# Attention with a gated FFN on one core: part of the third unit's row maxima by rectified differences on ScalarE, the last unit in halves, and another order table

## The chip, the cores and the metric

The kernel runs on one core of a Trainium2 chip. The metric is the device time of one execution in microseconds. Engines are named as in the profile: PE (TensorE), ACT (ScalarE), DVE (VectorE), POOL (GpSimd), SP (SyncE, which only issues DMAs here).

## The reference

A layer norm without weights, attention of 32 heads of 16 columns over 2048 rows, and a gated FFN on the raw input, summed with the input. `B_x` is not used.

```python
x = A_x                                   # [1, 2048, 512] bf16
xn = _layernorm(x, axis=-1)
# _A_ref: qkv = xn @ wqkv, 32 heads of 16
scores = jnp.einsum("bhqd,bhkd->bhqk", q, k) * (Dh ** -0.5)
p = _softmax(scores, axis=-1)
o = jnp.einsum("bhqk,bhkd->bhqd", p, v)   # then @ wo
# _B_ref: (silu(x @ w1) * (x @ w3)) @ w2, 1792 columns in between
return x + _A_ref(xn, A_wqkv, A_wo) + _B_ref(xn, B_w1, B_w3, B_w2)
```

## The kernel before, in words

**Units.** The 2048 rows of queries are four chunks of 512, the 32 heads eight groups of four. For each chunk and group the rows are cut into units: 128, 128 and 256 rows in the first, 128 four times in the last four groups, 256 twice elsewhere (`UNIT_HEAD`, `UNIT_TAIL`). There are 73 units, numbered from 0. "The third unit" is unit 2 (256 rows, head group 0, chunk 0), the last is unit 72 (128 rows).

**First pass, the row maxima.** For every 128 rows and head (a row block) PE makes scores against 2048 keys as four tiles of 128 by 512, one PSUM bank each (L1476, four heads side by side in the row groups of the array). DVE reduces two banks at a time to two maxima (`tensor_reduce`, L1529) and puts them in `part`, an SBUF tensor with one set of columns for even units and one for odd units. When a unit's maxima are all there, `final_max` takes the greatest over the four key chunks, on DVE for the first two and the last units (L1688) and on POOL otherwise (six short steps from L1658 on), and writes its negative, split in two bf16 numbers, into `Z`. From there it becomes two more rows of the transposed queries `QT`: through PE and one copy by ACT or DVE (`tile_QT2`, L1135 and L1131, the units in `FAST_AUG`), or through a transposing DMA and two more DMAs. So the second pass subtracts the maximum inside the matmul.

**Twelve row blocks go another way** (`SPLITS`, kind "S" in the list `p1`). With a and b the scores of two key chunks, max(a, b) = b + relu(a - b). POOL writes the negated queries `QN` (L1552), PE adds a and -b up in one bank (`d_cand`, L1588, twice, for chunks 0 and 1 and for 2 and 3), ACT writes the Relu of each bank into the buffer `RB` (L1597; two at once in `exp_pair`), PE makes b alone for chunks 1 and 3, and one DVE instruction adds `RB` and takes the maximum of all 1024 columns (L1522). That is one DVE instruction of two banks for a row block where the plain way takes two. A split counts as 2 in the progress count `p1_n`, like the four plain tiles that it stands for (0.5 each).

**Second pass.** PE makes the transposed scores against the augmented queries (L1796, or as full-width products with the block-diagonal `BD`, L835), ACT takes the exponential out of one bank (L1821) or of two neighbouring banks at once (L1852, "a pair") into slots of `PT`, PE multiplies with the values and a column of ones (`tile_PV`, L839), ACT copies the result out (L1919), POOL and some DMAs divide by the sum; for the last four units DVE does that (L1901 to L1905).

**Around it.** At the head the input is normalised (statistics on DVE and ACT by `STATS`, the scaling on DVE at L902 or on POOL at L912 by `NORM`, for eight groups of 128 rows times two), transposed on PE, copied out by ACT (L944), and multiplied for keys, queries and values. The keys of head group 0 come as four chunks KT0_0 to KT0_3 (`tile_KT`, evacuated by ACT at L968). The other groups' keys go through DRAM in pairs of groups (`tile_heads`: kq L1023, spill L994, fetch L1011), each with a point of `p1_n` by which it is needed (`HEAD_K`, `LEAD_K`). The FFN's tiles, the output products and the stores fill in between.

**The order** of all instructions is worked out while the program is built: `_Prog` keeps a model of each engine's time, and a loop at the end of `_build` takes, of the best candidates of the five engines, the one that the model starts first. Which candidate is best hangs on some forty numbers in `RULES` (K). The count of work done is cut into stretches of 12 (`SEG`); `TUNE` names for each stretch an entry of `SETS`, whose numbers replace the defaults there. In the first pass `p1_cand` takes the blocks of units 0 to 2 in any order as their keys arrive (`N_HEAD`), and the rest in the order of the list. A DVE or ACT instruction waits for what it reads and writes through semaphores; each engine runs its own list in order.

**The tail.** The last unit's 16 tiles of exponentials wait for its maxima; its output rows then need PV (L839), the division on DVE, the last output products (L835) and a store (L1250). `HALVES` (by `NHALF`, 0 before) names units whose heads 2 and 3 have their maxima, their augmented queries and their exponentials ahead of those of heads 0 and 1 (`half_max`, `qt_half`).

Of the kernel before, what the change touches and what calls it, by code (L numbers as in the profile page):

```python
# [268 lines left out]
def _build(nc, A_x, A_wqkv, A_wo, B_w1, B_w3, B_w2, out):  # L269
# [29 lines left out]
    NHALF = 0  # L299
# [11 lines left out]
    FFN_HI = 880  # L311
# [3 lines left out]
    HEAD_K = 14  # L315
# [8 lines left out]
    NORM = "dddppppp"  # L324
    STATS = "daddddaa"
    W2_AT = 8
    R_STAT = 2
    R_SEC = 1
    SPLITS = ((20, 44, 2), (58, 58, 2))
# [3 lines left out]
        dict(),  # L333
        dict(P2_FRAG=0.0, URG_WAIT=0.05, A_LEAD=0.82, PAIR_WAIT=0.15),
        dict(PAIR_WAIT=0.15, RELAX=0.05),
        dict(ROW_LEAD=0.4, P2_NEAR=0.2),
        dict(A_LEAD=0.69, P1_EARLY=0.15, COUPLE=0.25),
        dict(TOL=0.1),
        dict(TOL=0.15, TEN_MID=2),
        dict(TOL=0.0, PV_LEFT=2, A_LEAD=0.55, AGAIN=3),  # L340
        dict(A_LEAD=0.88, HEAT_WIDE=0.34, URG_WAIT=0.05),
        dict(TOL=0.15, BD_NEAR=0.8),
        dict(BD_NEAR=0.5, HEAT_P1=0.35, P1_SLIP=0.3, LAZY_MAX=6.0),
        dict(PV_LEFT=2, BD_NEAR=0.1),
# [10 lines left out]
        dict(P1_SLIP=0.15, BD_NEAR=0.5, RELAX=0.05, HEAT_TILE=0.5),
        dict(PAIR_TEN=2, ROW_LEAD=0.5),
        dict(P1_SLIP=0.3),
        dict(BD_NEAR=0.2, OUT_GATE=20, TOL=0.1),
        dict(PV_LEFT=2, TOL=0.1, LAZY_MAX=6.0, W_WAIT=0.1),
        dict(PAIR_DEPTH=5, P1_SLIP=0.15, COUPLE=0.25),  # L360
        dict(P1_SLIP=-0.15, WIDE_LEAD=1.0),
        dict(HEAT_FILL=0.6, P1_SLIP=-0.15),
        dict(HEAT_FILL=0.82, W_WAIT=0.2, SP_RANK=1),
        dict(BD_NEAR=0.1, OUT_GATE=20, P1_SLIP=0.15, P2_MID=5),
        dict(RELAX=0.1, HEAT_TILE=0.7, P1_SAME=-0.1),
        dict(HEAT_FILL=0.42, MIN_PIECE=2, W_WAIT=0.2, P2_MID=5),
        dict(PAIR_WAIT=0.1, BD_NEAR=0.5),
        dict(MIN_PIECE=3, PAIR_DEPTH=2, P1_TRI=1, PAIR_TEN=2),
        dict(OUT_GATE=14, TOL=0.1),
        dict(MIN_PIECE=3, P1_TRI=1, PACE=3000),  # L370
        dict(PAIR_WAIT=0.05, HEAT_FORCE=0.34, ROW_LEAD=0.5),
        dict(A_LEAD=0.88, P2_FRAG=0.2, P2_NEAR=0.1, HEAT_FORCE=0.0),
        dict(TOL=0.0, URG_WAIT=0.05, RELAX=0.05, AGAIN=1),
        dict(A_LEAD=0.69, WIDE_LEAD=1.0),
        dict(PAIR_DEPTH=5, HEAT_TILE=0.5, PAIR_WAIT=0.15),
        dict(COUPLE=0.04, P2_MID=2),
        dict(TOL=0.05),
        dict(BD_NEAR=0.5, WIDE_LEAD=0.7),
        dict(A_LEAD=0.69, HEAT_P1=0.35, HEAT_WIDE=0.0, WIDE_LEAD=1.0),
        dict(LAZY_MAX=6.0, BD_NEAR=0.1),  # L380
        dict(MIN_PIECE=2),
        dict(A_LEAD=0.55, PV_LEFT=3, FILL_SLIP=0.1, TOL=0.03),
        dict(A_LEAD=0.69, HEAT_FILL=0.82, URG_WAIT=0.15),
        dict(HEAT_WIDE=0.3, PAIR_WAIT=0.1, LAZY_MAX=1.0, P1_SLIP=0.15),
        dict(BD_NEAR=0.8),
        dict(PAIR_WAIT=0.0, A_LEAD=0.6, LAZY_GAP=0.3, P1_SAME=0.05),
        dict(A_LEAD=0.55, P1_TRI=1),
        dict(W_WAIT=0.2, COUPLE=0.08, HEAT_WIDE=0.57),
        dict(HEAT_P1=0.35, AGAIN=4, FILL_SLIP=0.2),
        dict(ROW_LEAD=0.4, TOL=0.15),  # L390
        dict(HEAT_FORCE=0.46, TRI_WAIT=0.3),
        dict(COUPLE=0.25, P1_SAME=0.1, ROW_LEAD=0.5),
        dict(TOL=0.1, SP_RANK=1, P1_TRI=1, COUPLE=0.25),
        dict(RELAX=0.2, P1_SLIP=-0.15),
        dict(A_LEAD=0.55, URG_WAIT=0.15),
        dict(PAIR_WAIT=0.1, HEAT_P1=0.35, URG_WAIT=0.15, SP_RANK=1),
        dict(P1_SLIP=0.3, SP_RANK=1, ROW_LEAD=0.55, P2_MID=2),
        dict(TOL=0.03, WIDE_LEAD=0.7, P2_NEAR=0.4),
        dict(ROW_LEAD=0.43, WIDE_LEAD=0.7),
        dict(FILL_SLIP=0.2, W_WAIT=0.2),  # L400
        dict(HEAT_P1=0.0, HEAT_FILL=0.82),
        dict(MIN_PIECE=2, TOL=0.05, WIDE_LEAD=0.7, W_WAIT=0.1),
        dict(FILL_SLIP=0.1, W_WAIT=0.1, P2_NEAR=0.02, WIDE_LEAD=1.0),
        dict(ROW_LEAD=0.55, PV_LEFT=2, HEAT_FILL=0.7, PAIR_WAIT=0.0),
        dict(TOL=0.03, P2_NEAR=0.0),
        dict(WIDE_LEAD=0.7, SP_RANK=1),
        dict(A_LEAD=0.69, SP_RANK=1, RELAX=0.1),
        dict(HEAT_FILL=0.75, ROW_LEAD=0.55, COUPLE=0.08),
        dict(P1_TRI=1, A_LEAD=0.82, P1_EARLY=0.3, WIDE_LEAD=1.0),
        dict(BD_NEAR=0.2, HEAT_TILE=0.5, URG_WAIT=0.05),  # L410
        dict(URG_WAIT=0.15, P1_SLIP=-0.15),
        dict(HEAT_FORCE=0.5, P2_NEAR=0.02),
# [198 lines left out]
    with ctx:  # L611
# [1881 lines left out]
```

## Time and profile before

| what | value |
|---|---|
| time, median of 3 runs | 1180.53 us (1180.08 to 1181.3) |
| span of the profiled execution | 1178.6 us |
| mean granted TensorE clock | 0.998 |
| first reduction of maxima begins, last begins | 13.79 us, 1160.97 us |
| first exponential begins, last ends | 36.62 us, 1173.3 us |
| busy DVE, ACT, PE, POOL | 1165.0, 1158.5, 1111.9, 449.4 us |

How to read the profile: a line of the page or of a view has the kernel's line (L1529), the engine, the operation, output and input tensors, shapes, the count, then the busy time and the mean length of one in ns, then the idle time of that engine just before and what ended it. A timeline has start and length in us; where several instructions are merged ("x17") the length runs from the first start to the last end. Instructions of one engine overlap a little, so the spacing of starts is less than the length of one; the chain of waits has lengths by spacing. In the row of digits each is the busy share of a fortieth of the span, in tenths.

### The profile page before, as it was taken

To read this page: it belongs to the slowest core of one execution; us is meant where nothing else is said; L and a number is where in the kernel's file an instruction comes from. 1 tells how busy PE (TensorE), PEld (TensorE's weight loads), DVE (VectorE), ACT (ScalarE), POOL (GpSimd) and SP (SyncE) were. 2 spreads that over 40 slices of the span, in tenths; PEclk is the share of its full clock that TensorE was granted. 3 is DMA by queue.
4 is the path that set the end of the run, shared out by engine and by line. 5 is a ranking of instruction groups with operands and counts; after the bars stand their busy time and mean duration, and the time that the engine had idled before them with its cause. 6 is when DMAs were issued, how large, how long until landed. Compare 5 with 4: busy or idle time off the path is not lost.

```text
span 1178.6 us, 35702 instructions
## 1 busy us (share of the span) xinstructions
PE 1111.9 (94%) x14770; PEld 512.0 (43%) x14922; DVE 1165.0 (99%) x1089; ACT 1158.5 (98%) x2130; POOL 449.4 (38%) x886
## 2 busy tenths in 40 slices
PE   8999999999999999999989999999999999899988
PEld 4444334434344433334434444434444443356654
DVE  8999999999999999999999999999999999999996
ACT  8899999999999999999999999999999999999998
POOL 7245534244424246244432222455632126432211
PEclk9999999999999999999999999999999999999999
DMA  8323232111121121111110111221210121001001
GB/s 250 82 70 80 61 91 58 48 29 40 31 49 32 31 67 35 46 39 30 45 27 24 30 43 28 60 52 44 54 30 22 43 57 36 25 22 29 11 11 28
DMA packets 140966, 55.79 MB, mean 47 GB/s; under 512 B 103296, under 2 KB 140804, under 8 KB 140804
## 3 DMA queue, kind: packets, MB, share of 16 engines
q1 hardware_dynamic: 140804, 53.50, 17.7%
q8 instruction: 118, 1.93, 0.7%
q14 instruction: 44, 0.36, 0.1%
HBM read 38.93 MB, written 6.74 MB: 39 GB/s over the span
## 4 chain that ended last, share of the span: by engine, by line
ACT 55%; DVE 31%; PE 11%; issue 1%; DMA 0%; POOL 0%; ACTq 0%; SPq 0%
ACT PT L1821 35%; DVE part L1529 31%; ACT PT L1852 13%; PE ps L835 4%; PE ps L839 3%; PE ps L1796 3%; PE ps L1476 2%; ACT zg L1191 1%; ACT ub L1195 1%; ACT th L1185 1%; ACT RB L1597 1%; ACT U L1919 1%; ACT kq L1023 0%; DMA PT<-in_A_x_dram 0%; ACT osb L1264 0%
## 5 line engine op out<-in xcount | busy, mean ns | idle before, releaser
L1529 DVE TENSOR_REDUCE part<-ps 128x2 f32<-128x1024 f32 x1000 | 1133.9, 1207 | 0.4 <-PE ps L1796 0.2
L1821 ACT ACTIVATE PT<-ps 128x512 bf16<-128x512 f32 x1498 | 799.6, 660 | 2.6 <-PE ps L1796 2.0
L1796 PE MATMUL ps<-QT,KT 32*128 32x256 bf16 (+1 forms) x3768 | 455.1, 258 | 9.0 <-ACT PT L1852 2.8
L1476 PE MATMUL ps<-KT,QT 32*128 32x512 bf16 x2048 | 417.1, 383 | 5.6 <-DVE part L1529 2.1
L1852 ACT ACTIVATE PT<-ps 128x1024 bf16<-128x1024 f32 x275 | 292.2, 1097 | 0.2
L1796 PEld LDWEIGHTS ps<-QT,KT 32*128 32x128 bf16 x3768 | 167.2, 92 | 164.0 <-issue 71.5
L839 PE MATMUL ps<-PT,Vaug 128*17 128x256 bf16 (+1 forms) x4672 | 185.5, 261 | 5.0 <-ACT PT L1852 2.7
L835 PE MATMUL ps<-xnT,ident 128*128 128x512 bf16 (+3 forms) x569 | 151.9, 324 | 24.5 <-ACT PT L1852 7.3
L1476 PEld LDWEIGHTS ps<-KT,QT 32*128 32x128 bf16 x2048 | 104.4, 91 | 141.8 <-issue 59.4
L835 PE MATMUL ps<-xnT,w 128*128 128x512 bf16 (+3 forms) x542 | 141.5, 330 | 8.3 <-ACT U L1919 2.3
L1944 POOL TENSOR_TENSOR Rc<-Lc,mone 128x8 f32<-128x8 f32 (+1 forms) x69 | 104.8, 1519 | 91.6 <-DMA Lc<-U 91.6
L839 PEld LDWEIGHTS ps<-PT,Vaug 128*17 128x17 bf16 x4672 | 88.0, 89 | 75.6 <-issue 51.1
L835 PE MATMUL ps<-BD,KT 128*128 128x256 bf16 (+1 forms) x604 | 103.6, 262 | 0.9 <-ACT PT L1852 0.3
L1658 POOL TENSOR_TENSOR mx<-part 128x16 f32<-128x16 f32 (+1 forms) x60 | 14.2, 236 | 233.9 <-DVE part L1529 233.7
L835 PEld LDWEIGHTS ps<-xnT,ident 128*128 128x128 bf16 x626 | 49.2, 97 | 105.2 <-ACT PT L1821 37.6
L835 PE MATMUL ps<-w,hT 128*128 128x128 bf16 (+3 forms) x326 | 77.9, 304 | 2.3 <-issue 1.0
L1162 POOL TENSOR_SCALAR t<-th 128x512 f32<-128x512 bf16 x56 | 34.7, 620 | 100.8 <-ACT th L1185 99.2
L835 PEld LDWEIGHTS ps<-xnT,w 128*128 128x128 bf16 x584 | 43.1, 97 | 67.4 <-issue 33.3
L1166 POOL TENSOR_TENSOR hT<-a,t 128x512 bf16<-128x512 f32 x56 | 71.0, 1268 | 2.5
L1164 POOL TENSOR_TENSOR a<-zg,ub 128x512 f32<-128x512 bf16 x56 | 64.5, 1153 | 7.5 <-ACT ub L1195 7.5
L835 PEld LDWEIGHTS ps<-BD,KT 128*128 128x128 bf16 x604 | 50.6, 98 | 22.5 <-ACT PT L1852 2.2
L1980 POOL TENSOR_TENSOR on_b<-U,R 128x256 bf16<-128x256 f32 (+1 forms) x33 | 23.4, 710 | 93.6 <-DMA R<-rd 93.5
(114 smaller groups left out, 722.8 us busy)
## 6 DMA issues: line engine op xcount, KB each, us to landing
w<-in_B_w_dram SPq DMA_DIRECT2D x112, 128.0 KB
R<-rd SPq DMA_DIRECT2D x55, 128.0 KB
QT<-qd SPq DMA_DIRECT2D x31, 128.0 KB
KT<-kd SPq DMA_DIRECT2D x28, 128.0 KB
BD<-QT SPq DMA_DIRECT2D x220, 10.5 KB
xr<-in_A_x_dram SPq DMA_DIRECT2D x16, 128.0 KB
out_dram<-osb SPq DMA_DIRECT2D x16, 128.0 KB
qd<-kq SPq DMA_DIRECT2D x15, 128.0 KB
```

Of the source, the lines that this page charges most:

```text
L835: return e.matmul(bank(bk)[:, c0 + a:c0 + b], make_lhsT(0, 128), rhs_ap(0)[:, a:b], start=start, stop=stop, **kw)
L839: ins = e.matmul(bank(bk)[32 * i:32 * i + m, c0 + a:c0 + b], make_lhsT(i), rhs if (a, b) == (0, ncols) else rhs[:, a:b], start=start, stop ...
L1162: q.append(_Item(lambda e: e.tensor_scalar(t1[:, :], th[:, ss, :], 1.0, 1.0, ALU.mult, ALU.add), [("th", ss)], [("t1",)], 0.62, 0.72))
L1164: q.append(_Item(lambda e: e.tensor_tensor(a32[:, :], zg[:, ss, :], ub[:, ss, :], ALU.mult), [("zg", ss), ("ub", ss)], [("a32",)], 1.1, 1.25))
L1166: q.append(_Item(lambda e: e.tensor_tensor(hT[:, hslot(idx), :], a32[:, :], t1[:, :], ALU.mult), [("a32",), ("t1",)], [("hT", hslot(idx))] ...
L1476: ins = e.matmul(bank(held[i]), QT[32 * j:32 * j + 32, qs, q * 128:(q + 1) * 128], KT[32 * j:32 * j + 32, g, c_ * 512:(c_ + 1) * 512], sta ...
L1529: redq.append(_Item(lambda e: e.tensor_reduce(dst, banks, AX.X, ALU.max), writes, [("part", par, i_) for i_ in ix[:m]], _c_dve(512 * m), c ...
L1796: ins = e.matmul(bank(b)[:, i * nq:(i + 1) * nq], KT[32 * j:32 * j + 32, g, (k0 + i) * 128:(k0 + i + 1) * 128], QT[32 * j:32 * j + 32, qs, ...
L1821: expq.append(_Item(lambda e: e.activation(PT[:, sl, :], bank(b), ACTF.Exp, scale=SCALE), [("ps", b)], [("PT", sl)], _c_act(512), cb=cb, e ...
L1852: return _Item(lambda e: e.activation(PT[:, s0:s1 + 1:s1 - s0, :], two_banks(b0, b1), ACTF.Exp, scale=SCALE), [("ps", b0), ("ps", b1)], [( ...
L1944: poolq["nrm"].append(_Item(lambda e: e.tensor_tensor(Rc[:, pp, 0:nl], Lc[:, pp, 0:nl], mone[:, 0:nl], ALU.pow), [("Lc", pp), ("mone",)], ...
L1980: poolq["nrm"].append(_Item(lambda e: e.tensor_tensor(onorm[ob][:, oslot(ob, g), q0:q0 + nq], U[:, us, 0:nq], R[:, pp, 0:nq], ALU.mult), [ ...
```

## The change

- `SPLITS`: the twelve steady row blocks by differences are in units 14 to 47, every third, where they were in units 20 to 42, every second.
- `HEAD_SPLITS`: five of the eight row blocks of unit 2 go by differences too. They come last in that unit's list; the other three stay plain and in the head's free order. There are three more buffers beside `RB`, in slots of `hT` that the FFN fills later; `HEAD_LOOK` and `split_prep` let their differences start up to 24 and their negation up to 40 counts ahead. One negation serves all blocks of the same 128 rows.
- Unit 2's maxima have columns of their own in `part` (`side`).
- `NHALF` = 1: the last unit in halves.
- The fourth of eight normalisation groups is scaled on DVE, not POOL; `HEAD_K` 14 to 8; transposes and the first group's keys get the rank of the augmented queries on PE (`FIRST`). `KT_PARTS` only makes a number out of what was fixed before.
- A second tile may be open for PV when slots of `PT` run out (`PV_TEN`, 0 by default). `OUT_GATE` 14 to 10, `FFN_HI` 880 to 900.
- The model's length of a split's DVE instruction grows by 0.028 us.
- New `SETS` and `TUNE`.

```diff
-    NHALF = 0
+    NHALF = 1
...
-    FFN_HI = 880
+    FFN_HI = 900
...
-    HEAD_K = 14
+    HEAD_K = 8
...
-    NORM = "dddppppp"
+    NORM = "ddddpppp"
...
+    KT_PARTS = (0,)
+    FIRST = ("AQ", "tr", "KT0")
...
-    SPLITS = ((20, 44, 2), (58, 58, 2))
+    SPLITS = ((14, 50, 3),)
+    SPLIT_ROWS = 1
+    HEAD_SPLITS = {2: ((0, 0), (0, 1), (0, 2), (0, 3), (1, 0))}
+    HEAD_BUFS = (10, 14, 18)
+    HEAD_LOOK = 24
...
+        PV_TEN=0,
...
-        OUT_GATE=14,
+        OUT_GATE=10,
...
+    SPLIT.update(HEAD_SPLITS)
...
-        part = sb("part", [128, 2, 8 * NQC], FP32)
+        part = sb("part", [128, 3, 8 * NQC], FP32)
...
+            rbufs = [(RB[:, :, :], [("RB", 0), ("RB", 1)], [[("RB", 0)], [("RB", 1)]])]
+            for s_ in HEAD_BUFS:
+                rbufs.append((hT[:, s_:s_ + 4, :].rearrange("p a b -> p (a b)").bitcast(FP32)
+                              .rearrange("p (h n) -> p h n", n=512), [("hT", s_ + i) for i in range(4)],
+                              [[("hT", s_), ("hT", s_ + 1)], [("hT", s_ + 2), ("hT", s_ + 3)]]))
...
+        def side(u):
+            return 2 if u == 2 else u % 2
...
             for k, (qt, j) in enumerate(split):
+                if u in HEAD_SPLITS:
+                    ops.append(("S", u, qt, 0, j))
+                    continue
...
-        N_HEAD = sum(1 for b_ in p1 if b_[1] < 3)
+        N_HEAD = sum(1 for b_ in p1 if b_[1] < 3 and b_[0] == "R")
...
+        split_buf = [k % len(rbufs) if p1[n][1] in HEAD_SPLITS else 0 for k, n in enumerate(splits)]
...
-                par = u % 2
+                par = side(u)
...
+                    rb, rk, _ = rbufs[split_buf[splits.index(n)]]
                     redq.append(_Item(lambda e: e.tensor_tensor_reduce(
-                        out=RB[:, :, :], in0=banks, in1=RB[:, :, :], scale=1.0, scalar=-BIG,
+                        out=rb, in0=banks, in1=rb, scale=1.0, scalar=-BIG,
...
-                        _c_dve(1024) + 0.06, cb=fired, pred=lambda: split_done[n][0] == 2))
+                        writes + rk, rk + [("part", par, ix[0])],
+                        _c_dve(1024) + 0.088, cb=fired, pred=lambda: split_done[n][0] == 2))
...
+            ahead = 40 if u in HEAD_SPLITS else 16
...
-            if p1_at[n] - p1_n[0] > K.SPLIT_LOOK or (k and not split_done[splits[k - 1]][2]):
+            bf, kn = split_buf[k], split_of[k] % 2
+            if (p1_at[n] - p1_n[0] > (HEAD_LOOK if p1[n][1] in HEAD_SPLITS else K.SPLIT_LOOK)
+                    or any(split_buf[k_] == bf and not split_done[splits[k_]][2] for k_ in range(k))):
...
+            tenants = sum(b in bank_tenant for b in pool_banks())
+            if (p2_n[0] and red_n[0] < NP1 and tenants == K.TEN_MID and len(pt_free) <= K.PV_TEN and pv_ready()
+                    and not any(t.name.startswith("PV") for t in bank_tenant.values())):
+                bk = free_bank()[0]
...
-            return 0 if t.name.startswith("AQ") else 1.5 if t.name.startswith("V") else 2 if t.name.startswith("OUTB") else 1
+            return 0 if t.name.startswith(FIRST) else 1.5 if t.name.startswith("V") else 2 if t.name.startswith("OUTB") else 1
```

More of the change, by code (lines that the diff above doesn't have):

```diff
@@ L355, in _build @@
[L355 to L364, printed above, removed]
@@ L513, in _build @@
[L513 to L521 removed]
+        dict(COUPLE=0.18, HEAT_FILL=0.5),
@@ L599, in _build @@
     NU = len(units)
-    SPLIT = {u: ((units[u][3] // 128 - 1, 3),) for lo, hi, st in SPLITS for u in range(lo, hi, st)}
+    SPLIT = {u: tuple((units[u][3] // 128 - 1, 3 - r) for r in range(SPLIT_ROWS)) for lo, hi, st in SPLITS for u in range(lo, hi, st)}
+    SPLIT.update(HEAD_SPLITS)
     FAST_AUG = {0, 1} | set(range(NU - NFAST, NU))
@@ L952, in tile_KT @@
             groups = []
-            if sc == 0:
-                for t in range(XG):
+            if sc in KT_PARTS:
+                for t in range(4 * sc, 4 * sc + 4):
                     for c in range(DC):
@@ L971, in evac @@
                               cb=lambda op: done.add(("KT", 0, sc)), name="first")]
-            return _Tile("KT0_%d" % sc, groups, evac, cols=2048 if sc else 512,
+            return _Tile("KT0_%d" % sc, groups, evac, cols=512 if sc in KT_PARTS else 2048,
                          pred=lambda: "wk0" in done
-                         and all(("xnT", t) in done for t in range(sc * 4, sc * 4 + (4 if sc else 1))))
+                         and all(("xnT", t) in done for t in range(sc * 4, sc * 4 + (1 if sc in KT_PARTS else 4))))
         kq_free = list(range(NKQ))
@@ L1331, in _build @@
         NP1 = p1_at[-1]
-        N_HEAD = sum(1 for b_ in p1 if b_[1] < 3)
+        N_HEAD = sum(1 for b_ in p1 if b_[1] < 3 and b_[0] == "R")
+        assert all(b_[0] == "R" for b_ in p1[:N_HEAD])
         ug_n = {}
@@ L1544, in split_prep @@
             ug = qc * NG + g
-            if p1_at[n] - p1_n[0] > 16 or ("QT", ug) not in done or (i >= 2 and split_done[splits[i - 2]][1] < 2):
+            ahead = 40 if u in HEAD_SPLITS else 16
+            if (p1_at[n] - p1_n[0] > ahead or ("QT", ug) not in done or (u in HEAD_SPLITS and "QTb" not in done)
+                    or (i >= 2 and any(split_done[m_][1] < 2 for k_, m_ in enumerate(splits) if split_of[k_] == i - 2))):
                 return
@@ L1624, in final_max @@
             na = 4 * nqt
-            keys = [("part", par, i_) for i_ in range(NQC * na)]
-            p4 = part[:, par, 0:NQC * na].rearrange("p (k a) -> p a k", a=na)
+            keys = [("part", side(u), i_) for i_ in range(NQC * na)]
+            p4 = part[:, side(u), 0:NQC * na].rearrange("p (k a) -> p a k", a=na)
             ng = negm[:, par, 0:4 * nqt]
@@ L1653, in pool_max @@
                             1.0, 0.0, ALU.mult, ALU.add),
-                        [("part", par, i0)], [("part", par, i0 + na * c_) for c_ in range(1, 4)], 0.22))
+                        [("part", side(u), i0)], [("part", side(u), i0 + na * c_) for c_ in range(1, 4)], 0.22))
                 d2, m2 = mx[:, 0, 0:4 * nqt, :], mx[:, 1, 0:4 * nqt, :]
@@ L1695, in half_max @@
             par = u % 2
-            keys = [("part", par, 4 * c_ + j) for c_ in range(NQC) for j in js]
+            keys = [("part", side(u), 4 * c_ + j) for c_ in range(NQC) for j in js]
             h = slice(js[0], js[-1] + 1)
-            p4 = part[:, par, 0:4 * NQC].rearrange("p (k a) -> p a k", a=4)[:, h, :]
+            p4 = part[:, side(u), 0:4 * NQC].rearrange("p (k a) -> p a k", a=4)[:, h, :]
             ng = negm[:, par, h]
```

388 lines of the change are left out of this document (197 added, 191 removed), and 24 rows, old and new, of the table TUNE.

## The prediction

> **What bounds the kernel now.** I read the page first, then the busy time by stretch, the groups by shape, the two ends of the span as timelines, and the chain of waits.
>
> ```profile
> PE 1111.9 (94%) x14770; PEld 512.0 (43%) x14922; DVE 1165.0 (99%) x1089; ACT 1158.5 (98%) x2130; POOL 449.4 (38%) x886
> DVE  8999999999999999999999999999999999999996
> ACT  8899999999999999999999999999999999999998
> L1529 DVE TENSOR_REDUCE part<-ps 128x2 f32<-128x1024 f32 x1000 | 1133.9, 1207 | 0.4 <-PE ps L1796 0.2
> L1821 ACT ACTIVATE PT<-ps 128x512 bf16<-128x512 f32 x1498 | 799.6, 660 | 2.6 <-PE ps L1796 2.0
> L1852 ACT ACTIVATE PT<-ps 128x1024 bf16<-128x1024 f32 x275 | 292.2, 1097 | 0.2
> ```
>
> Two engines are full. DVE spends nearly all of it on one thing, the row maxima: 1000 reductions of two banks each, with 0.4 us of idle time ahead of all of them. ACT spends it on exponentials, 1498 of one bank and 275 of two. So the question is which of the two ends later once work is moved between them, and where each has holes.
>
> ```profile
> 25.00:35.00 10.00, 9.95 (x63) 3.82 (x62) 9.96 (x11) 5.94 (x10) 8.08 (x9) 1.00 0.59 187
> 35.00:60.00 25.00, 24.20 (x257) 11.66 (x264) 24.97 (x24) 22.96 (x45) 2.27 (x11) 1.00 0.30 77
> 60.00:100.00 40.00, 39.00 (x528) 17.95 (x529) 40.00 (x36) 39.19 (x72) 19.79 (x33) 1.00 0.28 68
> 100.00:500.00 400.00, 379.88 (x4609) 161.47 (x4649) 400.00 (x359) 398.48 (x714) 162.94 (x305) 1.00 0.20 50
> 500.00:1100.00 600.00, 568.50 (x7501) 262.02 (x7575) 599.76 (x542) 598.14 (x1108) 226.30 (x457) 1.00 0.15 37
> 1100.00:1173.30 73.30, 66.43 (x1655) 41.82 (x1665) 66.91 (x79) 73.00 (x137) 13.62 (x28) 1.00 0.08 17
> 1173.30:1178.60 5.30, 2.07 (x19) 0.59 (x20) 1.79 (x5) 0.00 (x0) 0.00 (x0) 0.55 0.07 25
> ```
>
> The columns after the stretch are its length and the busy time of PE, PE's weight loads, DVE, ACT and POOL, then the granted clock. ACT's holes are length minus busy: 4.06 us in 25 to 35, then 2.04, 0.81, 1.52, 1.86 and 0.30, 10.59 us in all until its last exponential at 1173.3. DVE has 0.31 us from 25 to 1100. The final 5.3 us hold only the last unit's products, its division and the store; nothing in the change touches them.
>
> ```profile
> 1160.97 1.21 DVE L1529 TENSOR_REDUCE part<-ps 128x2 f32<-128x1024 f32 x1
> 1164.11 0.28 DVE L1131 TENSOR_SCALAR QT<-ps 128x128 bf16<-128x128 f32 x1
> 1164.30 2.00 ACT L1852 ACTIVATE PT<-ps 128x1024 bf16<-128x1024 f32 x2
> 1169.35 3.92 ACT L1852 ACTIVATE PT<-ps 128x1024 bf16<-128x1024 f32 x4
> ```
>
> The last maximum ends at 1162.2, its result stands in QT at 1164.4, and the ACT timeline from 1164.30 on has eight pairs and three singles, 19 tiles, the last unit's 16 and three left over. ACT had about one microsecond of backlog when DVE delivered, so the two limits now coincide: **DVE sets the pace, and ACT is only about 1 us from setting it itself.** A change has to move both.
>
> **The change, part by part.** *Five row blocks of the third unit by rectified differences.* A row block is four maxima over 512 columns, two of L1529's reductions. The other way, in use on twelve blocks now, takes two one-bank Relus on ACT and one two-bank sum with maximum on DVE.
>
> ```profile
> 15.11 19.22 DVE part L1529 x17
> 676.90 10.78 ACT PT L1821 x22
> 222.73 3.67 ACT PT L1852 x4
> ```
> ```profile
> 366.10 1.21 DVE L1522 CUSTOM_DVE_ANT_0 RB<-ps,RB 128x1024 f32<-128x1024 f32 x1
> 367.24 0.08 DVE L1522 DVE_READ_ACCUMULATOR2_ANT part<- 128x1 f32 x1
> 367.24 2.35 DVE L1529 TENSOR_REDUCE part<-ps 128x2 f32<-128x1024 f32 x2
> L1597 ACT ACTIVATE RB<-ps 128x512 f32<-128x512 f32 x24 | 15.3, 646 | 0.1
> ```
>
> Instructions overlap, so I use spacings, not durations. A reduction takes 19.22/17 = 1.131 us of DVE; the split's one takes 367.24 - 366.10 = 1.14, and the next reduction starts while its accumulator is read. Per block DVE saves 2 x 1.131 - 1.14 = 1.12 us, for five 5.6. A one-bank ACT operation takes 10.78/22 = 0.49 us, a pair 3.67/4 = 0.917; the Relus have the shape of the exponentials, so ten cost 4.9 us (4.6 if all pair up).
>
> [...]
>
> Where do they lie? At the head, where ACT has its largest hole.
>
> ```profile
> 18.76 0.69 ACT L968 ACTIVATE KT<-ps,kbias 128x512 bf16<-128x512 f32 x1
> ...
> 30.08 0.69 ACT L968 ACTIVATE KT<-ps,kbias 128x512 bf16<-128x512 f32 x1 [0.69 <-PE ps L835]
> ...
> 36.62 1.02 ACT L1852 ACTIVATE PT<-ps 128x1024 bf16<-128x1024 f32 x1
> ```
> ```profile
> 50.65 0.24 POOL L1658 TENSOR_TENSOR mx<-part 128x16 f32<-128x16 f32 x1 [13.05 <-DVE part L1529]
> 50.98 0.20 POOL L1659 TENSOR_SCALAR mx<-mx 128x16 f32<-128x16 f32 x1
> ```
> ```profile
> 54.96 0.65 SPq L994 DMA_DIRECT2D kd<-kq  x1
> ...
> 58.01 1.44 SPq L1011 DMA_DIRECT2D KT<-kd  x2
> ```
>
> The second of the four key chunks is there at 19.5, so five first halves (2.5 us) can go into the hole of 25 to 35; the second halves need the fourth chunk. It comes at 30.8 and the first exponential at 36.6, so they go between. I take the hole as wholly filled: 4.06 of the 4.9 us are covered and 0.84 us are added to ACT. Without that cover all 4.9 would be added.
>
> The new wait: a split's sum needs both Relus, and DVE runs in order, so every later maximum queues behind it, and with it the banks those maxima hold on PE. The blocks come last in the unit and four buffers allow four at work, so I cost it at nothing, with at most one Relu spacing (0.49 us) for each of the last two as upper bound. PE gets six 512-column products per block where it had four: ten more at 0.37 us (below), side by side in row groups, against 0.8 us of PE idle in 35 to 60; they displace filling. POOL gets one more negation and five small copies ahead of the third unit's maxima, 0.33 us each by the spacing of the two steps above; it sat idle 13.05 us before that point.
>
> *Own columns for the third unit* remove no wait that the rows show (0.4 us before 1000 reductions), so zero; both ends of the bound are within that 0.4.
>
> *Fourth normalisation group on DVE, not POOL, and the head's ranks and key needs.*
>
> ```profile
> L902 DVE TENSOR_SCALAR osb<-PT,U 128x512 bf16<-128x512 bf16 x6 | 2.2, 407 | 0.0
> 25.38 1.52 POOL L912 TENSOR_SCALAR osb<-PT,U 128x512 bf16<-128x512 bf16 x2
> L1476 PE MATMUL ps<-KT,QT 32*128 32x512 bf16 x2048 | 417.1, 383 | 5.6 <-DVE part L1529 2.1
> ```
>
> DVE gets two of these, 2 x 2.2/6 = 0.7 us. POOL, which normalises until 26.9, is relieved of two (1.5 us) and two coefficient steps, so the fourth key chunk and the first exponential can come up to 1.5 us earlier, or not at all if ACT's other work holds them. I take no gain: an earlier start only shortens the hole that the Relus fill.
>
> The third unit's maxima end 5.6 - 0.7 = 4.9 us earlier, at about 45.7, and its exponentials can begin as much earlier, while ACT still has the 32 tiles of the first two units; that covers most of ACT's 2.85 us of holes in 35 to 100. What is late next is the second group's last key chunk: the fourth unit needs it 12 reductions (13.6 us) after its start, at 64.2 now and at 59.3 afterwards. Its load is issued at 58.01 and, going by the 3.05 us from its spill's issue (54.96) to its own, lands by 61.1. Left there, DVE would lose up to 1.8 us, of the gain and not beyond it; with HEAD_K at 8 these loads are due six steps (6.8 us) sooner, so I take zero.
>
> *Last unit in halves.* Only eight tiles wait for the last maximum, not sixteen: four pairs, 4 x 0.917 = 3.7 us off DVE's limit. It adds one small reduction (0.18 us, below) and one more copy like that of 1164.11 (0.28), on ACT or DVE. ACT's own limit does not move by it.
>
> ```profile
> 34.34 0.18 DVE L1688 TENSOR_REDUCE negm<-part 128x4 f32<-128x16 f32 x1
> ```
>
> *Steady blocks in units 14 to 47 by threes, for 20 to 42 by twos*: twelve either way, no cost. *Order*: the rules in SETS and TUNE only decide what comes when; I bound it by the pairs below.
>
> **The sum.** DVE's limit: -5.6 + 0.7 + 0.2 = -4.7, with the halves -8.4 us. ACT's limit: +4.9 for the Relus, -4.06 for the hole they fill, -2.6 for nine tenths of the 2.85 us in 35 to 100, and -1.8 for half of the 3.68 us after 100, where ACT waits on PE as often as on late maxima: -3.5 us. The later end decides: ACT, **-3.5 us**. The profiled span of 1178.6 becomes 1175.1; the median stands 1.9 us above that span, so I predict **1177.0 us**. At most, all 10.59 us of holes go and 4.9 come: -5.7, 1174.8. At least, only the hole at the head goes: +0.8, 1181.4.
>
> **The rivals.** *ACT's holes stay* (no change). L1821's 2.6 us of waiting is nearly all on PE, which is 95% busy in the middle, so DVE's freed time may turn into DVE idle time while ACT runs as before: between +0.8 and -2.0, 1178.5 to 1181.3. For it speaks that only 10.6 us of 1173 are to be had; against it, that 2.9 of them lie just where the third unit is late.
>
> *Fewer pairs* (slower). A pair saves 2 x 0.49 - 0.917 = 0.063 us, and its two banks must be neighbours and free together.
>
> ```profile
> 600.00:700.00 100.00, 14.86 (x14) 1.00 0.11 29
> 800.00:900.00 100.00, 38.98 (x36) 1.00 0.17 40
> ```
>
> These are the pairs (L1852) in two stretches of the same length, 14 and 36, so the order alone moves them by more than two to one. The gain is gone with 3.5/0.063 = 56 fewer than 275, and the time is slower by over 0.2% below 275 - 94 = 181; at 14 per 100 us throughout there would be about 150, +7.8 us on the forecast, 1184.8. Splits hold PSUM banks, which speaks for it; twelve steady ones before and after speaks against.
>
> *More pairs* (faster still). With 4.9 us of slack against ACT's limit (8.4 - 3.5), DVE can give banks away: 60 more pairs are -3.8, 1173.2.
>
> *PE's clock falls* (slower). It was granted at 1.00 in every stretch up to 1173.3 and at 0.55 in the last, where PE was busy 2.07 of 5.30 us. If the new filling rules leave PE that idle elsewhere, each microsecond at half clock loses half of PE's work; 12 us of it lose 6, 1183. Nothing in the rows comes near: the leanest stretch before is 91% busy. [...]
>
> *The halves do nothing*: ACT is the later one by my own sum, so this costs the forecast only if DVE gains less than 3.5 elsewhere; it is inside the range.
>
> **How the numbers follow.** A measurement of this kernel can tell about 0.2% (2.4 us) from no change. Forecast 0.60 (1174.8 to 1178.1), holes stay 0.22, more pairs 0.07, fewer pairs 0.09, clock 0.02. Faster is 0.67, the same 0.22, slower 0.11. The range runs from 1173.2 (25 pairs on top of the best sum) to 1181.0, near the worst end of the holes that stay; outside lie most of the fewer pairs, the clock and a little of the more pairs.
>
> **What would show it.** L1529 x990 and L1522 x17; ten Relus before about 40 us; ACT idle in 25 to 35 under 1 us; the third unit's POOL maxima near 46; the last unit's first half in QT some 4 us before the last maximum ends; DVE idle in the last 20 us that was not there before. I am wrong if ACT's holes after 35 us stay above 5 us, if the pairs move by more than 30, or if DVE still has the last word at the end.

## The result, and the profile after

| what | before | after |
|---|---|---|
| time, median of 6 runs each (lowest, highest) | 1180.51 us (1180.08 to 1181.3) | 1175.12 us (1174.93 to 1175.56) |
| span of the profiled execution | 1178.6 us | 1173.3 us |
| last maximum ends | 1162.2 us | 1159.3 us |
| last exponential ends | 1173.3 us | 1168.1 us |

The ratio after to before is 0.9944, interval 0.9927 to 0.9961: faster by 5.4 us, where 3.5 were forecast. In some runs of the experiments the mean granted clock was lower (down to 0.98 from 0.998) and the time longer (in experiment 4 1206.03 us at 0.981, 1187.76 at 0.998); experiments 4 and 7 have mostly such runs, so their profiled executions are read instead (4 at 0.998, 7 itself at 0.994).

The changed kernel's page shows its busy times and the three large groups; the old L1529, L1821 and L1852 are now L1546, L1842 and L1874:

```profile
PE 1126.4 (96%) x14755; PEld 510.0 (43%) x14755; DVE 1160.6 (99%) x1092; ACT 1159.1 (99%) x2115; POOL 450.4 (38%) x891
...
L1546 DVE TENSOR_REDUCE part<-ps 128x2 f32<-128x1024 f32 x990 | 1123.2, 1215 | 0.8 <-PE ps L1492 0.7
L1842 ACT ACTIVATE PT<-ps 128x512 bf16<-128x512 f32 x1446 | 778.5, 674 | 0.9 <-PE ps L1817 0.5
L1874 ACT ACTIVATE PT<-ps 128x1024 bf16<-128x1024 f32 x301 | 324.1, 1119 | 0.1
```

There are ten reductions fewer and 26 pairs more, and the idle time ahead of single exponentials is 0.9 us where it was 2.6. The busy time by stretch has the columns of the prediction's table:

```profile
25.00:35.00 10.00, 10.00 (x67) 3.98 (x65) 9.23 (x10) 6.58 (x14) 7.97 (x8) 1.00 0.48 146
35.00:60.00 25.00, 24.70 (x253) 11.31 (x251) 24.97 (x28) 24.30 (x45) 3.55 (x17) 1.00 0.26 70
60.00:100.00 40.00, 38.53 (x502) 16.38 (x503) 39.94 (x37) 40.00 (x72) 20.54 (x34) 1.00 0.30 73
100.00:500.00 400.00, 385.96 (x4754) 166.05 (x4753) 400.00 (x360) 399.87 (x710) 163.80 (x311) 1.00 0.19 49
500.00:1100.00 600.00, 579.50 (x7553) 260.74 (x7550) 600.00 (x542) 599.64 (x1102) 226.59 (x450) 1.00 0.15 37
1100.00:1168.10 68.10, 64.94 (x1451) 38.81 (x1450) 62.96 (x76) 68.03 (x131) 12.93 (x29) 1.00 0.07 15
1168.10:1173.30 5.20, 1.14 (x19) 0.41 (x18) 1.79 (x5) 0.00 (x0) 0.00 (x0) 1.00 0.15 50
```

ACT's holes (length minus busy) are 3.42, 0.70, 0.00, 0.13, 0.36 and 0.07 us, 4.68 in all against 10.59 before. The one that the prediction meant to fill, 25 to 35, went only from 4.06 to 3.42; all the later ones together went from 6.53 to 1.26. In that first stretch PE is busy 10.00 of 10.00 us. The ACT timeline shows what that does to the Relus (L1618; they write `RB` or the buffers in `hT`):

```profile
26.07 0.60 ACT L1618 ACTIVATE RB<-ps 128x512 f32<-128x512 f32 x1 [0.58 <-PE ps L1609]
...
30.42 0.69 ACT L971 ACTIVATE KT<-ps,kbias 128x512 bf16<-128x512 f32 x1 [0.69 <-PE ps L836]
32.14 0.60 ACT L1026 ACTIVATE kq<-ps 128x512 bf16<-128x512 f32 x1 [1.03 <-PE ps L836]
33.27 0.60 ACT L1618 ACTIVATE RB<-ps 128x512 f32<-128x512 f32 x1 [0.54 <-PE ps L1609]
...
37.01 0.60 ACT L1842 ACTIVATE PT<-ps 128x512 bf16<-128x512 f32 x1 [0.48 <-PE ps L1817]
37.50 0.59 ACT L1618 ACTIVATE hT<-ps 128x512 f32<-128x512 f32 x1
...
43.53 1.21 ACT L1618 ACTIVATE RB<-ps 128x512 f32<-128x512 f32 x2
```

Only two of the ten lie in the stretch, and seven come after the first exponential. Each idle time names PE, which makes keys, values and queries (L836), transposes and scores in that stretch. The DVE timeline has the rest of the head:

```profile
27.82 6.88 DVE L1546 TENSOR_REDUCE part<-ps 128x2 f32<-128x1024 f32 x6 [0.74 <-PE ps L1492]
...
40.71 1.21 DVE L1539 CUSTOM_DVE_ANT_0 RB<-ps,RB 128x1024 f32<-128x1024 f32 x1
...
45.34 1.22 DVE L1539 CUSTOM_DVE_ANT_0 RB<-ps,RB 128x1024 f32<-128x1024 f32 x1
46.48 0.08 DVE L1539 DVE_READ_ACCUMULATOR2_ANT part<- 128x1 f32 x1
```

The five sums (L1539) start 1.14 to 1.20 us apart, without a wait that the view names, so the new wait cost next to nothing. But DVE now waits 0.74 us at 27.08 for scores, a gap that was not there. At the end, in the same view:

```profile
1149.01 0.31 DVE L1923 STREAM_TRANSPOSE RB<-ps 128x128 f32<-128x128 f32 x1
...
1154.71 0.31 DVE L1923 STREAM_TRANSPOSE RB<-ps 128x128 f32<-128x128 f32 x1
...
1155.61 0.29 DVE L1927 TENSOR_TENSOR wk_on<-ps,R 128x128 bf16<-128x128 f32 x1
1155.82 3.48 DVE L1546 TENSOR_REDUCE part<-ps 128x2 f32<-128x1024 f32 x3
1159.33 0.17 DVE L1736 TENSOR_REDUCE negm<-part 128x2 f32<-128x8 f32 x1
```

The divisions of two units (L1923 to L1927, 1.11 us each, 1154.71 to 1155.82) stand ahead of the last maxima, where one did before. So the last maximum should be earlier by 5.61 (ten reductions of 1.131 less five sums of 1.14) - 0.72 (normalisation) - 0.74 (gap) - 1.11 (division), which is 3.0 us and close to the 2.9 of the table. The other 2.4 us lie behind it: 16.4 us from the last maximum to the end became 14.0.

### The profile page after: what moved, and what is told of

The parts are those of the page before. It is cut to its first block, busy times and chain, and to the rows that moved or that the text cites. A ratio compares the mean times of both kernels' runs of the same rounds, so it can differ in the third digit from the quotient of the medians.

```text
span 1173.3 us, 35501 instructions
## 1 busy us (share of the span) xinstructions
PE 1126.4 (96%) x14755; PEld 510.0 (43%) x14755; DVE 1160.6 (99%) x1092; ACT 1159.1 (99%) x2115; POOL 450.4 (38%) x891
## 4 chain that ended last, share of the span: by engine, by line
ACT 71%; PE 14%; DVE 13%; issue 1%; DMA 1%; SPq 0%
ACT PT L1842 45%; ACT PT L1874 16%; DVE part L1546 13%; PE ps L836 6%; PE ps L840 3%; PE ps L1817 3%; PE ps L1492 2%; ACT zg L1194 2%; ACT ub L1198 2%; ACT th L1188 2%; ACT U L1941 1%; ACT RB L1618 1%; ACT kq L1026 1%; DMA wk_on<-in_A_wqkv_dram 1%; ACT osb L1267 0%
## 5 line engine op out<-in xcount | busy, mean ns | idle before, releaser
L1546 DVE TENSOR_REDUCE part<-ps 128x2 f32<-128x1024 f32 x990 | 1123.2, 1215 | 0.8 <-PE ps L1492 0.7
L1842 ACT ACTIVATE PT<-ps 128x512 bf16<-128x512 f32 x1446 | 778.5, 674 | 0.9 <-PE ps L1817 0.5
L1492 PE MATMUL ps<-KT,QT 32*128 32x512 bf16 x2026 | 410.0, 384 | 4.5 <-DVE part L1546 1.7
L1874 ACT ACTIVATE PT<-ps 128x1024 bf16<-128x1024 f32 x301 | 324.1, 1119 | 0.1
L840 PE MATMUL ps<-PT,Vaug 128*17 128x256 bf16 (+1 forms) x4672 | 189.7, 261 | 2.5 <-DVE part L1546 0.6
L836 PE MATMUL ps<-xnT,ident 128*128 128x512 bf16 (+3 forms) x538 | 151.7, 338 | 17.8 <-DVE part L1546 6.1
L1492 PEld LDWEIGHTS ps<-KT,QT 32*128 32x128 bf16 x2026 | 101.4, 91 | 144.1 <-issue 75.3
L836 PE MATMUL ps<-xnT,w 128*128 128x512 bf16 (+3 forms) x609 | 151.4, 327 | 5.0 <-DVE part L1546 0.4
L836 PE MATMUL ps<-BD,KT 128*128 128x256 bf16 (+1 forms) x588 | 102.2, 263 | 0.0
L836 PEld LDWEIGHTS ps<-xnT,ident 128*128 128x128 bf16 x538 | 43.8, 97 | 96.4 <-ACT PT L1842 31.4
L836 PE MATMUL ps<-w,hT 128*128 128x512 bf16 (+3 forms) x349 | 82.6, 306 | 0.0
L836 PEld LDWEIGHTS ps<-xnT,w 128*128 128x128 bf16 x609 | 46.0, 97 | 69.8 <-issue 32.0
L840 PE MATMUL ps<-BD,KT 128*32 128x256 bf16 (+1 forms) x1280 | 58.3, 264 | 0.1
L836 PEld LDWEIGHTS ps<-BD,KT 128*128 128x128 bf16 x588 | 49.8, 98 | 19.9 <-ACT PT L1842 1.0
```

The lines of the kernel that those rows point to most:

```text
L836: return e.matmul(bank(bk)[:, c0 + a:c0 + b], make_lhsT(0, 128), rhs_ap(0)[:, a:b], start=start, stop=stop, **kw)
L840: ins = e.matmul(bank(bk)[32 * i:32 * i + m, c0 + a:c0 + b], make_lhsT(i), rhs if (a, b) == (0, ncols) else rhs[:, a:b], start=start, stop ...
L1492: ins = e.matmul(bank(held[i]), QT[32 * j:32 * j + 32, qs, q * 128:(q + 1) * 128], KT[32 * j:32 * j + 32, g, c_ * 512:(c_ + 1) * 512], sta ...
L1546: redq.append(_Item(lambda e: e.tensor_reduce(dst, banks, AX.X, ALU.max), writes, [("part", par, i_) for i_ in ix[:m]], _c_dve(512 * m), c ...
L1842: expq.append(_Item(lambda e: e.activation(PT[:, sl, :], bank(b), ACTF.Exp, scale=SCALE), [("ps", b)], [("PT", sl)], _c_act(512), cb=cb, e ...
L1874: return _Item(lambda e: e.activation(PT[:, s0:s1 + 1:s1 - s0, :], two_banks(b0, b1), ACTF.Exp, scale=SCALE), [("ps", b0), ("ps", b1)], [( ...
```

## The experiments

The first question was which engine has the last word. The prediction's theory is ACT alone, with DVE some 5 us ahead of it; the first rival is DVE alone.

**1 to 4: more work on one engine, nothing else changed.** Ten exponentials (or five reductions) are issued twice in a row, in the changed kernel and in the one before; the first issue counts on a semaphore of its own, which the engine waits for.

```diff
+            for _ in range(self.again.get(id(op), 0)):
+                op.fn(handle).then_inc(self.own, 1)
+                self.n_own += 1
+                handle.wait_ge(self.own, self.n_own)
             ins = op.fn(handle)
...
+        P.again = {id(op): 1 for op in [op for op in P.ops["act"] if op.name == "ex"][150:1400:125]}
```

> The changed kernel in its own order, with ten of its one-bank exponentials, spread evenly over the middle, done twice on ACT (the second waits for the first, about 0.7 us each, 7 us in all). The forecast's theory, that ACT has the last word after the change: 5 to 7 us longer than the changed kernel, about 1181. The rival, that DVE still sets the pace and ACT waits in many short pieces that the idle column does not show: under 2 us longer, 1175 to 1177.

> The changed kernel in its own order, with five of its reductions done twice on DVE (about 1.3 us each, 6.5 us in all). The forecast's theory: DVE has some 5 us of slack against ACT, so 0 to 2 us longer, 1175 to 1177. The rival: DVE is the pace, so 6 to 7 us longer, about 1181.5.

> The kernel before, with ten exponentials done twice on ACT (7 us in all). The forecast had ACT only 1 us away from setting the pace: 5 to 6 us longer, about 1186. The rival: under 2 us longer, 1180.5 to 1182.5.

> The kernel before, with five reductions done twice on DVE (6.5 us in all). Both theories have DVE as the pace here: 6 to 7 us longer, about 1187. Less than 4 would speak against both.

| run | median us | ratio to before (interval) | span, against its own kernel's |
|---|---|---|---|
| 1, changed, ACT | 1182.69 | 1.0005 (0.9993 to 1.0017) | 1180.6, +7.3 |
| 2, changed, DVE | 1182.73 | 0.9996 (0.9977 to 1.0015) | 1179.4, +6.1 |
| 3, before, ACT | 1187.19 | 1.0049 (1.0034 to 1.0064) | 1183.4, +4.8 |
| 4, before, DVE | 1192.78 | 1.0124 (1.0059 to 1.0189) | 1185.9, +7.3 |

Ten exponentials of 0.67 us are 6.7, five reductions of 1.215 are 6.1. In the changed kernel both come through whole, and the gain is gone (ratios 1.0005 and 0.9996): neither "ACT alone" nor "DVE alone" fits. By medians both are 7.6 us above the changed kernel's 1175.12. It was not run again beside them; the lowest time of the kernel before was 0.8 us higher there than at first (1180.84, 1180.08), so some of the 7.6 may be that. The groups of experiment 1, then of experiment 2 (a few lines were added above, so numbers are 4 higher), show the other engine standing still meanwhile:

```profile
L1550 DVE TENSOR_REDUCE part<-ps 128x2 f32<-128x1024 f32 x990 | 1125.6, 1214 | 5.5 <-PE ps L1496 2.6
L1846 ACT ACTIVATE PT<-ps 128x512 bf16<-128x512 f32 x1456 | 783.8, 670 | 2.1 <-PE ps L1821 1.1
```
```profile
L1550 DVE TENSOR_REDUCE part<-ps 128x2 f32<-128x1024 f32 x995 | 1129.3, 1227 | 0.9 <-PE ps L1496 0.7
L1846 ACT ACTIVATE PT<-ps 128x512 bf16<-128x512 f32 x1446 | 777.5, 672 | 3.2 <-PE ps L1821 2.3
L1878 ACT ACTIVATE PT<-ps 128x1024 bf16<-128x1024 f32 x301 | 323.4, 1114 | 2.5 <-PE ps L1821 1.6
```

More on ACT, and DVE's idle time rises from 0.8 to 5.5 us; more on DVE, and ACT's goes from 1.0 to 5.7 over both groups. (In the profiled execution of experiment 1 the clock was 0.50 from 210.22 to 213.63, and 1.1 of DVE's 5.5 us lie there; its executions at a mean clock of 1.00 were no shorter, 1182.43 to 1182.71 us against 1182.35.) In the kernel before, DVE's work comes through whole as well (+7.3) and ACT's but for about 2 us (+4.8 of 6.7). A new theory: the engines are held together through PE's list, which serves both in a fixed order.

**5 and 6: the halves alone.** `NHALF` back to 0 in the changed kernel, and to 1 in the one before.

```diff
-    NHALF = 1
+    NHALF = 0
```

> The changed kernel with the last unit whole again; all else, the order up to the last unit too, as it is. The forecast's theory (ACT last, its limit untouched by halves): no change, 1174.5 to 1175.7. The rival (DVE is the pace to its last maximum, then the last unit's exponentials follow): 2 to 4 us longer, 1177 to 1179.

> The kernel before with only its last unit in halves. The forecast's theory: at most the 1 us that DVE was later than ACT, 1179.5 to 1180.5. The rival: 2 to 4 us shorter, 1176.5 to 1178.5.

Without halves the changed kernel takes 1176.15 us (ratio 0.9948, 0.9928 to 0.9968), span 1174.4: they are worth 1.0 to 1.1 us there. In the kernel before there was no gain: 1182.09 us (ratio 0.999, 0.9964 to 1.0016), span 1180.5. Its order changed too (267 pairs for 275), so this run doesn't price the halves alone. Experiment 5's ACT timeline also shows what else the tail gained:

```profile
1158.90 1.57 ACT L1842 ACTIVATE PT<-ps 128x512 bf16<-128x512 f32 x3
1161.60 4.69 ACT L1874 ACTIVATE PT<-ps 128x1024 bf16<-128x1024 f32 x5 [1.13 <-PE ps L1817]
...
1167.52 1.65 ACT L1842 ACTIVATE PT<-ps 128x512 bf16<-128x512 f32 x3
```

Even without halves ACT has run dry when the last maximum arrives, and 16 tiles follow (1161.60 to 1169.17, 7.57 us), where before there were 19 (1164.30 to 1173.27, 8.97 us). From the last maximum (1159.4) to the end it has 15.0 us, against 16.4 before and 14.0 with the halves. So the smaller backlog goes with 1.4 us of the tail's 2.4, and the halves are the other 1.0.

**7: no differences in the third unit.** All else as changed, order table included.

```diff
-    HEAD_SPLITS = {2: ((0, 0), (0, 1), (0, 2), (0, 3), (1, 0))}
+    HEAD_SPLITS = {}
```

> The changed kernel without the five row blocks of the third unit by differences; the order behind the head comes out of the same table but differs. The forecast's theory: DVE gets 4.9 us more and ACT loses 4.9 us of Relus; ACT decides, so 0 to 2 us shorter or longer. The rival: DVE has 5.6 us more and 0.7 us less of waiting at the head, so 4 to 6 us longer, 1179 to 1181. The order itself may add 1 or 2 us to either.

The median is 1206.05 us (lowest 1199.98; ratio 1.02, 1.014 to 1.0261); the profiled execution's span is 1198.3, 25.0 above the changed kernel. Its groups:

```profile
L1546 DVE TENSOR_REDUCE part<-ps 128x2 f32<-128x1024 f32 x1000 | 1136.2, 1213 | 7.1 <-PE ps L1492 3.5
L1842 ACT ACTIVATE PT<-ps 128x512 bf16<-128x512 f32 x1704 | 905.8, 689 | 9.1 <-PE ps L1817 6.3
L1874 ACT ACTIVATE PT<-ps 128x1024 bf16<-128x1024 f32 x172 | 185.6, 1130 | 1.0 <-PE ps L1817 0.6
```

The differences themselves can account for 5.6 us of DVE. 129 pairs are lost (8.1 us of ACT at 0.063 each), since the counts of `TUNE` meet another course. And PE's clock fell to 0.50 twice for 6.83 us (from 824.95 and from 876.15); 4.5 of DVE's 7.1 us of waiting and 4.1 of ACT's 10.1 lie in these two stretches. What is left is put down to the order and is not shown apart. So this run does not price the differences; it prices a table that doesn't fit.

**8: the third unit's maxima in shared columns.**

```diff
-            return 2 if u == 2 else u % 2
+            return u % 2
```

> The changed kernel with the third unit's maxima in the first unit's columns again. Both theories: no wait of DVE hangs on it, so within 1 us of the changed kernel, 1174 to 1176. It also shows how far a small shift of the order alone moves the time, where it shifts.

The median is 1175.22 us (1174.96 to 1175.37; ratio 0.9938, 0.9914 to 0.9962), span 1173.4: zero either way, as forecast.

**9 to 12: less work, order unchanged.** If two engines are held together, a cut on one gains nothing and a cut on both does. At each cut an instruction reads only 64 of 512 columns, and the kernel leaves the others out. The last run puts both cuts at the same eight places.

```diff
+            self.cut_now = id(op) in self.cut
...
-                    dst, banks, AX.X, ALU.max),
+                    dst, banks[:, :, 0:64] if P.cut_now else banks, AX.X, ALU.max),
...
-                expq.append(_Item(lambda e: e.activation(PT[:, sl, :], bank(b), ACTF.Exp, scale=SCALE),
+                expq.append(_Item(lambda e: e.activation(PT[:, sl, 0:64] if P.cut_now else PT[:, sl, :],
+                                                         bank(b)[:, 0:64] if P.cut_now else bank(b), ACTF.Exp, scale=SCALE),
```

> The changed kernel with its order as it is; 21 exponentials of one bank, spread from the 150th to the 1400th, read 64 of their 512 columns (the other columns of those tiles are left out). A pair's spacing is 0.904 us and a single's 0.477, so a bank of 512 columns costs 0.427 and 448 columns 0.37: about 7.8 us less on ACT. If ACT alone has the last word, as the prediction had it, the time falls by 5 to 8 us to about 1169. If the two engines are held together and DVE never waits (its spacing exceeds 1.131 us by only 1.3 us in all), nothing is gained: 1174.0 to 1175.6, and the freed time shows as ACT's idle time.

> The changed kernel with its order as it is; eight of the 990 reductions, spread, read 64 of 512 columns of each of their two banks (the rest is left out), about 7 us less on DVE. If DVE alone has the last word and ACT's hidden short waits (31 us by spacing) are slack, the time falls by all of it, to about 1168. If ACT alone has the last word (the prediction), nothing: 1174.5 to 1175.6. If the two are held together, the time falls by what ACT's short waits can give, I take 1 to 3 us: 1172 to 1174.

> Both cuts in one kernel. If the two engines are held together, only this one falls by more than 4 us, to 1168 to 1171, though neither cut alone does. If ACT alone has the last word, it ends where the cut on ACT alone does; if DVE alone has, where the cut on DVE alone does.

> The changed kernel with its order as it is, and both cuts at the same eight places: at each, one reduction reads 64 of 512 columns of each bank (measured before: 281 ns instead of 1215, about 0.93 us less), and the three exponentials of one bank that run in the same two microseconds read 64 of 512 columns (about 0.37 us less each, 1.1 us). The other columns of those tiles are left out. If DVE and ACT are held together step by step, with room for only about one tile between them, the cuts now fall into the same steps and nearly all of DVE's 7.5 us shows: 1167.5 to 1170. If PE is a third limit with no room of its own, the gain stays near that of the cuts at different places (1.5 us): 1172 to 1174. If either engine alone set the pace, one of the two single cuts would have shown it already.

| run | median us (lowest to highest) | ratio to before (interval) | span |
|---|---|---|---|
| 9, ACT less | 1175.05 (1174.81 to 1175.17) | 0.9913 (0.9875 to 0.9951) | 1173.4 |
| 10, DVE less | 1175.06 (1174.83 to 1175.3) | 0.9928 (0.9904 to 0.9953) | 1173.5 |
| 11, both, apart | 1173.59 (1173.17 to 1173.89) | 0.9912 (0.988 to 0.9943) | 1171.8 |
| 12, both, same places | 1174.02 (1173.79 to 1174.37) | 0.992 (0.9889 to 0.9952) | 1172.2 |

Against the changed kernel's 1175.12 the single cuts gain nothing, so ACT alone and DVE alone both fall. (It was not run beside them, but experiment 8, which costs nothing, took 1175.22 in another set of runs; experiments 9, 10 and 11 ran beside each other.) Together the cuts gain only 1.5 us, and at the same places 1.1, not the 4 to 8 that I expected of two engines bound to each other: that form of my theory fell too. Where the freed time went stands in the groups of experiments 9, 10 and 12, in this order:

```profile
L1547 DVE TENSOR_REDUCE part<-ps 128x2 f32<-128x1024 f32 x990 | 1123.0, 1215 | 0.8 <-PE ps L1493 0.7
L1843 ACT ACTIVATE PT<-ps 128x512 bf16<-128x512 f32 (+1 forms) x1446 | 770.3, 654 | 4.0 <-PE ps L1818 1.5
```
```profile
L1547 DVE TENSOR_REDUCE part<-ps 128x2 f32<-128x1024 f32 x990 | 1117.3, 1208 | 5.7 <-PE ps L1493 3.0
L1843 ACT ACTIVATE PT<-ps 128x512 bf16<-128x512 f32 x1446 | 778.6, 675 | 0.8 <-PE ps L1818 0.5
```
```profile
L1547 DVE TENSOR_REDUCE part<-ps 128x2 f32<-128x1024 f32 x990 | 1116.6, 1208 | 6.4 <-PE ps L1493 3.7
L1843 ACT ACTIVATE PT<-ps 128x512 bf16<-128x512 f32 x1446 | 768.4, 655 | 5.8 <-PE ps L1818 3.3
```

The engine that has less to do waits for PE instead: ACT's idle time goes from 0.9 to 4.0, DVE's from 0.8 to 5.7, and with both cut they reach 5.8 and 6.4. Two of the eight places in experiment 12, by stretch (length, then busy PE, PEld, DVE, ACT, POOL), with the sum over all eight, and the same of the changed kernel:

```profile
298.00:304.00 6.00, 5.80 (x101) 2.51 (x93) 5.40 (x6) 5.41 (x14) 2.37 (x9) 1.00 0.17 51
...
771.00:777.00 6.00, 6.00 (x108) 2.92 (x111) 5.28 (x6) 5.42 (x13) 5.75 (x7) 1.00 0.16 47
...
sum 48.00, PE 47.39 PEld 20.00 DVE 42.39 ACT 43.28 POOL 24.66; mean PE 5.92 PEld 2.50 DVE 5.30 ACT 5.41 POOL 3.08
```
```profile
298.00:304.00 6.00, 6.00 (x109) 2.50 (x97) 6.00 (x7) 6.00 (x13) 2.39 (x9) 1.00 0.19 55
...
771.00:777.00 6.00, 5.67 (x92) 2.81 (x93) 6.00 (x6) 6.00 (x12) 5.50 (x6) 1.00 0.16 48
...
sum 48.00, PE 46.99 PEld 19.83 DVE 48.00 ACT 48.00 POOL 23.30; mean PE 5.87 PEld 2.48 DVE 6.00 ACT 6.00 POOL 2.91
```

Uncut, DVE and ACT are busy all 48.00 us and PE 46.99. With both cut, DVE and ACT fall to 42.39 and 43.28 and PE stays at 47.39. So PE had 1.0 us of idle time in all at these places, and the gain was 1.1: its list, score tiles and filling alike, is as full there as the others. **Three engines are full in the changed kernel, in one fixed order.** The added delays on DVE or ACT were not made up; time taken off either, or off both, turned into a wait for PE. Two limits of this reading: PE's busy time is rough (1126.4 us in the changed kernel's profile and 1104.9 in experiment 1's, with 14755 weight loads in both), and no run takes work off PE, so that PE is the third limit is read from the waits and not tested. Away from these places PE isn't wholly full either: between 100 and 1100 it is idle 34.5 us, and the view of its waits puts 20.9 of them down to ACT or DVE.

## Why the prediction was right, and which of its steps failed

The direction held, and the time is inside the range, 1.9 us below the forecast. The mechanism held only in part: no single engine ends later and decides. That the sum came so near is partly luck, since its errors had both signs: the hole at the head was taken 3.4 us too well, and the later holes, the pairs and the short waits some 5 us too badly. Step by step:

- *"ACT is only about 1 us from setting it itself. A change has to move both."* The coincidence was real, experiments 3 and 4 show it: in the kernel before, extra work costs 4.8 us on ACT and 7.3 on DVE. "The later end decides: ACT" failed: experiments 1, 2, 9 and 10 show no single later end. PE, whose added products were only to "displace filling", is the third limit in the changed kernel as far as its waits show. The rows for it stood there: PE busy 9.95 of 10.00 us in 25 to 35.
- *The hole of 25 to 35 "as wholly filled"*: this is the largest term that failed. 0.64 of 4.06 us went. I asked which keys had come, not when PE could make the difference products (L1609); two of ten Relus lie in the hole.
- *Half of the holes after 100 us, 1.8, and nine tenths of 35 to 100, 2.6*: measured 3.12 and 2.15. The first was too small, and nothing in the runs says whether the freed DVE or the new table did it.
- *Pairs*: bounded at 30, they moved by 26, 1.6 us off ACT at the prediction's price (1.3 by distances of starts, 0.477 and 0.904 us); the sum had none. The terms as measured (+4.9 - 0.64 - 2.15 - 3.12 - 1.6) give -2.6, while ACT's last exponential ends 5.2 us earlier. Summed from its first exponential to its last, ACT's time above the usual distance of starts for each shape fell by 7.7 us, from about 36 to 29, of which only 5.8 and 0.5 show as idle time. So up to 2.5 us of what the sum lacks are waits too short to show; a nanosecond in the usual distance moves this by 1.6 us.
- *DVE's limit, -4.7*: it measured -2.9 at the last maximum. The five differences gave their 5.6; missing in the sum were the 0.74 us gap at 27.08 and a second division of 1.11 us ahead of the last maxima.
- *Halves, -3.7 on DVE's limit and nothing on the time*: they were worth 1.0 us in the changed kernel (experiment 5). They do take half the last exponentials from behind the last maximum, but from 1157.9 to 1168.6 the chain of waits is PE's, so most of the 3.7 was not to be had.
- *Own columns, zero*: shown by experiment 8. *The new wait, nothing*: the five sums run in a row. *Keys of the second group*: they do not hold up the fourth unit, DVE's idle time in 35 to 60 is 0.03 us as before; their loads are issued at 42.50 and 49.26, before at 48.44 and 58.01.
- *The Relus at 0.49 us* held. The last exponentials, copies and Relus of the head start 0.47 to 0.48 apart (42.10, 42.57, 43.05, 43.53 in the ACT timeline), and after four of the Relus (37.50, 38.45, 39.09, 41.62) the next instruction starts 0.47 to 0.48 later.
- *"Fewer pairs" and "PE's clock falls", as rivals*: neither happened here, but experiment 7 has both, 129 pairs fewer and 13.7 us at a clock of 0.50, in its 25 us. The rival ties the fall to an idle PE, which is not shown: in the kernel before the clock fell to 0.50 at 1173.80, after 5.00 us in which PE was busy 2.97, and in the changed kernel, with PE busy 1.14 of the last 5.20 us, it stayed at 1.00. That half the clock loses half of PE's work was an estimate: in the kernel before, the three products of 128x512 at 0.50 lasted 610 to 634 ns, ten of the same at 1.00 just before 379 to 389.
- *The signs*: the counts came (990 and 17), and POOL's maxima of the third unit start at 46.92 (50.65 before). Three signs failed: ACT is idle 3.42 us in 25 to 35 where under 1 was expected, four of the ten Relus start after 40 us, and the last unit's first half stands in QT at 1156.75, 2.6 us ahead of the last maximum's end and not 4.

What stays open: whether PE was already the third limit before (there the extra work was tried, the cuts were not), and how the 5.3 us divide between the parts and the new table. PE's 94% before does not speak against it: that profile has 14770 products for 14922 weight loads, so the records of 152 products are missing, while experiment 6, the kernel before with halves, has all 14942 and shows PE busy 96%, as in the changed kernel. The new table without the other parts was not run, so it may account for much of the gain. Taking the differences out of this table costs far more than they can be worth (experiment 7); the pieces that come apart are 1.0 us for the halves and zero for the columns.

## What to carry to other kernels

When two engines read 99% and a third 96%, ask for each not only what its list costs but whether the engine that feeds it could deliver earlier: a cut of some 7.5 us on each of two engines was worth 1.5 us here, and the feeder had hardly any idle time at the places of the cuts (1.0 of 48 us). The cheap test is a pair of runs with the order left alone, some work doubled on one engine and some cut: a single limit would show in both, and here only the added work did. And a hole in the busy row can be filled only by work whose inputs can be made in time: look at the feeding engine in the same stretch first.

## What the runs showed of the hardware

- Idle time understates waiting on ACT. A one-bank operation lasts 0.67 us in the groups and starts 0.48 after the one before, so by an estimate from these two a wait of up to some 0.2 us between two of them doesn't show. In the changed kernel about 29 us lie above the usual spacing, and 0.5 of it shows as idle.
- PE's busy time of two profiles isn't to be compared closely. The changed kernel shows 14755 products and 1126.4 us; experiment 1, with the same 14755 weight loads, shows 14603 products and 1104.9 us.
- PE's granted clock at the very end differs between executions: 1.00 for the changed kernel, 0.79 for experiment 12 over the same last 5.2 us, 0.55 for the kernel before, with no difference of length that follows it (5.2, 5.2 and 5.3 us). It fell at one moment to 0.50: at 1173.80 in the kernel before, at 1169.99 in experiment 12, and in the changed kernel not before its end at 1173.3.
- In the middle it fell to 0.50 once for 3.41 us (experiment 1) and twice for 6.83 (experiment 7). In 824.95 to 831.78 of experiment 7, PE shows as busy 6.83 of 6.83 us while DVE is busy 4.19 and ACT 4.75, so there the time at the lowered clock showed as idle on DVE (2.64 us) and ACT (2.08) and not on PE.
